# All matrix products in 64x64 array tiles, in pairs that exchange their row halves

## The chip, the cores and the metric

One core of a Trainium2 chip runs the kernel. TensorE (PE) multiplies, ScalarE (ACT) and VectorE (DVE) empty its results from the eight PSUM banks, GpSimd (POOL) and SyncE (SP) issue DMAs. The metric is the device time of one execution in microseconds (us), as a median of several runs.

## What is computed

Attention without a softmax, and then an MLP mixer over its result; 8 batch items, 12 heads, 448 tokens, 64 channels a head.

```python
def _attn_ref(q, k, v):
    S = q.shape[2]
    scale = 1.0 / np.sqrt(q.shape[-1])
    scores = scale * np.matmul(q, k.transpose(0, 1, 3, 2))
    attn = np.maximum(scores, 0.0) ** 2 / S
    return np.matmul(attn, v)
# x: the heads side by side, (8, 448, 768)
def _moe_ref(x, w_tok1, w_tok2, w_ch1, w_ch2):
    xt = x.transpose(0, 2, 1)
    h = np.maximum(xt @ w_tok1, 0.0) @ w_tok2      # 448 -> 256 -> 448
    u = x + h.transpose(0, 2, 1)
    h2 = np.maximum(u @ w_ch1, 0.0) @ w_ch2        # 768 -> 1536 -> 768
    return u + h2
```

Inputs and output are float32; the kernel computes in bfloat16 with float32 sums.

## The kernel before

The 96 pairs of batch item and head are worked off in 24 steps of four heads (`NS`), three steps to a batch item. Tokens are numbered as seven blocks of 64 (`KC`, `KP`): token 7p + c is place p of block c.

The stages of a step, with the names that the planner and the lines carry:

- T (L526): q and k are transposed, on PE in the first nine steps, by DMA later.
- S (L577): scores of one token block for four heads, four matmuls in 64x64 array tiles ("a quad"), into two banks. ACT or DVE take the relu (L309, L311), DVE squares (L611).
- V (L629): the product with v, 7 quads, into two banks; scaled into `xT` (L659, L661).
- X: x is transposed back to token rows, on PE in the first six steps (L714), by DMA later.
- t1 (L751): first token product, full 128x128 matmuls of 256 columns, tokens padded to 512 so that each of four K steps has 128 rows. Relu into `r1`.
- t2 (L786): second token product, one bank for each of two head pairs; DVE adds x and writes `uT` (L798).

Then, per batch item, come the channel products: C1 (L842), for each of 12 output blocks six accumulating 128x128 matmuls of 448 columns into one bank, then a relu into `r2` (L309); and C2 (L913), for each of 28 x 2 output tiles twelve matmuls of 384 columns into one bank, then DVE adds u (L947), and SP stores the result. A chain of C1 or C2 is one unit that nothing interrupts.

What sets the order: each operation of each stage is an `Op` with dependencies, duration, number of banks and rank, and a `Planner` walks through a model of time and gives out the operations, engine by engine. The program then runs in this fixed order, with semaphores between the engines. The model reckons 0.093 us for a change of PE's tile shape (`shape` "s" for 64x64, "m" for 128x128), and so runs several S or V operations on end (`run`, `WAIT`) before it goes to the full-size units, and begins such a run only with enough free banks (`OPEN`, `SPARE`). Loads on POOL are a fixed list. Small matmuls on a tile of zeros (L432, L436) keep PE busy in the first 16 us.

Of the kernel before, what the change touches and what calls it, by code (L numbers as in the profile page):

```python
# [17 lines left out]
WAIT, SPARE, OPEN = 0.1, 1, 6  # L18
# [5 lines left out]
class Op:  # L24
    def __init__(self, name, eng, emit, deps=(), **kw):
        self.name, self.eng, self.emit = name, eng, emit
        self.deps = [d for d in deps if d is not None]
        self.on = None
        self.start = self.seen = None
        self.banks = 0  # L30
        self.bank = []
        self.frees = None
        self.rank = 0
        self.shape = None
        self.lag = 0.0
        self.work = None
        self.late = None
        self.durs = None
        self.batch = None
        self.step = 0  # L40
        self.spare = 0
        self.gate = None
        self.first = self.then = None
        self.__dict__.update(kw)
# [5 lines left out]
class Planner:  # L50
# [10 lines left out]
    def done(self, o):  # L61
        for d in o.users:
            d.left -= 1
            d.at = max(d.at, o.seen)
            if d.left == 0:
                self.open[d.pool].append(d)

    def run(self, todo, reserve, least, lanes=8, held=0.0, fill=None):
        for n, o in enumerate(self.ops):
# [3 lines left out]
            o.pool = "FLEX" if o.durs else "UNIT" if o.shape == "m" else "PE" if o.shape else o.eng  # L73
# [11 lines left out]
        banks = [0.0] * 7 + [held]  # L85
        ring = 0.0
        landed = {"POOL": [], "SP": []}
        todo = list(todo)
        shape, owed, run = None, 0.0, False
# [6 lines left out]
        idle = 0.0  # L96
        while left:
            for e in ("SP", "POOL"):
# [23 lines left out]
                left -= 1  # L122
            for e in ("ACT", "DVE"):
# [23 lines left out]
                o.emit(o)  # L147
                self.log.append((t, e, o.name, o.durs[e]))
# [5 lines left out]
            if free["PE"] <= t:  # L154
                o = None

                def fits(c, spare=0):
                    at = t + (0.093 if shape not in (None, c.shape) else 0.0)
                    return c.ready(at) and sum(b <= at for b in banks) >= c.banks + max(spare, c.spare if c.then and c.then.left > 1 else 0)

                pick = None
                for u in self.open["UNIT"]:
                    if fits(u) and (pick is None or (u.rank, u.n) < (pick.rank, pick.n)):
                        pick = u
                spare = 0 if pick is None else SPARE
                head = todo[0] if todo else None
                if head and head.step < TIGHT and not head.ready(t):
                    head = next((u for u in todo[1:LOOK] if u.ready(t)), head)
                if pick is not None and pick.rank < 0:
                    o = pick  # L170
                    run = False
                elif run and head and fits(head, spare):
                    o = head
                elif run and head and idle < WAIT:
                    pass
                else:
                    run = False
                if o is None and not run:
                    if pick is None:
                        o = next((u for u in todo[:12] if fits(u)), None)  # L180
                    elif head and owed <= 0.0 and fits(head, max(0, OPEN - head.banks)):
                        o = head
                    else:
                        o = pick
                if o is None:
                    idle += step
                else:
                    at = t + (0.093 if shape not in (None, o.shape) else 0.0)
                    idle = 0.0
                    if o.shape == "m":  # L190
                        owed = max(owed - o.dur, -2.0)
                    else:
                        run = True
# [13 lines left out]
                    for k in order:  # L207
                        banks[k] = 1e9
                    self.open[o.pool].remove(o)
# [12 lines left out]
def kernel(  # L222
# [22 lines left out]
    SP = 512  # L245
# [9 lines left out]
    EARLY1, EARLY2, SPARE1 = 3, 3, 3  # L255
# [10 lines left out]
    xTs = [sbuf.tile([128, 2, SP], BF16, name=f"xT{i}") for i in range(NX)]  # L266
    wt1 = sbuf.tile([128, 4, DT], BF16, name="wt1")
# [7 lines left out]
    x_sbs = [sbuf.tile([128, 2, 4, 128], BF16, name=f"x_sb{i}") for i in range(2)]  # L275
# [4 lines left out]
    outs = sbuf.tile([128, NO, DM], FP32, name="out_sb")  # L280

# [6 lines left out]
    VFROM, ASPLIT = 3, 3  # L288
# [18 lines left out]
    def relu(o, out, ps):  # L307
        if o.on == "ACT":
            nc.scalar.activation(out, ps, AF.Relu)  # L309
        else:  # L310
            nc.vector.tensor_scalar(out=out, in0=ps, scalar1=0.0, scalar2=None, op0=ALU.max)  # L311

    def copy(o, out, ps):
        if o.on == "ACT":
            nc.scalar.activation(out, ps, AF.Copy)
        else:
            nc.vector.tensor_copy(out, ps)  # L317

    def freed(u, i=None):
        return lambda o: u.bank if i is None else [u.bank[i]]  # L320

# [55 lines left out]
    def load_wt1():  # L377
        w = moe_w_tok1.rearrange("(p c) j -> c p j", c=KC)
        got = []
        for c2 in range(2):  # L380
            n = (KC + 1 - c2) // 2

            def emit(o, c2=c2, n=n):
                nc.gpsimd.dma_start(
                    out=wt1[64 * c2 : 64 * (c2 + 1), :n, :],
                    in_=w[c2::2].rearrange("c p j -> p c j"),
                )

            got.append(add(Op(f"wt1.{c2}", "POOL", emit, dur=0.6, work=0.9)))
        return got  # L390
# [50 lines left out]
    nc.vector.memset(wt1, 0.0)  # L441
    for x in xTs:
        nc.vector.memset(x[:, :, S:], 0.0)

# [175 lines left out]
    def value(s):  # L620
# [35 lines left out]
        def evict(o, half):  # L656
            dst = xTs[s % NX][:, half, :S]
            if o.on == "ACT":
                nc.scalar.activation(dst, u.ps[half][:, :S], AF.Copy, scale=float(alpha2))  # L659
            else:  # L660
                nc.vector.tensor_scalar(  # L661
                    out=dst, in0=u.ps[half][:, :S], scalar1=float(alpha2), scalar2=None, op0=ALU.mult
# [22 lines left out]
    def mixing(s):  # L685
# [4 lines left out]
        if s >= XDMA:  # L690
# [5 lines left out]
                        out=x_sb.rearrange("p a c d -> p (a c) d"),  # L696
                        in_=xTs[s % NX].rearrange("p a n -> p (a n)"),
# [6 lines left out]
            ready = xback[s] * 2  # L704
        else:
            ready = [None, None]
            xback[s] = []
            for lo, hi in ((0, 1), (1, 2)) if s < ASPLIT else ((0, 2),):

                def emit_x(o, lo=lo, hi=hi):  # L710
                    o.ps = bank(o, 0, "x_ps").bitcast(BF16).rearrange("p (a c d) -> p a c d", a=2, c=4)
                    for a in range(lo, hi):
                        for c in range(4):
                            nc.tensor.matmul(  # L714
                                o.ps[:, a, c, :],
                                lhsT=xTs[s % NX][:, a, c * 128 : (c + 1) * 128],
                                rhs=ident,
# [6 lines left out]
                u = add(Op(f"X{s}.{lo}", "PE", emit_x, xe[s][lo:hi], shape="m", banks=1, dur=0.22 * (hi - lo), rank=1))  # L724
                xback[s].append(u)
                units.append(u)
                n = 512 * (hi - lo)
                cp = add(
                    Op(
                        f"xc{s}.{lo}",  # L730
                        "DVE",
                        lambda o, lo=lo, hi=hi, u=u: copy(o, x_sb[:, lo:hi], u.ps[:, lo:hi]),
                        [u] + old,
                        durs={"ACT": 0.05 + n / 1200, "DVE": 0.067 + n / 1920},
                        slack=0.4,
                        rank=1,
                        frees=freed(u),
                    )
                )
                for a in range(lo, hi):  # L740
                    ready[a] = cp

        r1 = r1s[s % 2]
        t1e[s], r1_op = [], [None, None]
        for lo, hi in ((0, 1), (1, 2)) if s < ASPLIT else ((0, 2),):

            def emit_1(o, lo=lo, hi=hi):
                o.ps = bank(o, 0, "t1_ps").rearrange("p (j n) -> p j n", j=JC)
                for j in range(JC):
                    for c in range(4):  # L750
                        nc.tensor.matmul(  # L751
                            o.ps[:, j, lo * 128 : hi * 128],
                            lhsT=wt1[:, c, j * 128 : (j + 1) * 128],
                            rhs=x_sb[:, lo:hi, c, :],
                            start=(c == 0),
                            stop=(c == 3),
                        )

            t1 = add(
                Op(f"t1.{s}.{lo}", "PE", emit_1, ready[lo:hi] + wt1_ops, shape="m", banks=1, dur=0.436 * (hi - lo), rank=1)  # L760
            )
            t1e[s].append(t1)
            units.append(t1)
            n = 256 * (hi - lo)
            ev = add(
                Op(
                    f"r1.{s}.{lo}",
                    "ACT",
                    lambda o, lo=lo, hi=hi, t1=t1: relu(
                        o, r1[:, :, lo * 128 : hi * 128], t1.ps[:, :, lo * 128 : hi * 128]  # L770
                    ),
                    [t1] + [ue.get((s - 2, a)) for a in range(2)],
                    durs={"ACT": 0.05 + n / 1200, "DVE": 0.067 + n / 960},
                    slack=0.3,
                    rank=0,
                    frees=freed(t1),
                )
            )
            for a in range(lo, hi):
                r1_op[a] = ev  # L780
        for a in range(2):

            def emit_2(o, a=a):
                o.ps = bank(o, 0, "h_ps")
                for j in range(JC):
                    nc.tensor.matmul(  # L786
                        o.ps[:, :S],
                        lhsT=r1[:, j, a * 128 : (a + 1) * 128],
                        rhs=wt2[:, j, :],
                        start=(j == 0),  # L790
# [272 lines left out]
```

## Time and profile before

| what | us |
|---|---|
| median of 3 runs (358.99 to 359.59) | 359.37 |
| the profiled execution | 359.65 |
| its span, first to last instruction | 357.8 |
| PE busy | 351.8 |
| DVE busy | 232.5 |
| ACT busy | 202.0 |
| POOL busy | 84.3 |

The span leaves out 1.85 us of the profiled execution. Busy is the time in which an instruction of the engine runs; matmuls overlap in the record, so PE's 351.8 says that it nearly always had work, not how fast it went. The costliest stages on PE by busy time are C2 (115.2 us), C1 (115.0), S (48.0) and V (37.2). The DMA engines' mean busy share is nine tenths or more in nearly all of the first three quarters of the span.

### The profile page before, as it was taken

The page shows a single profiled execution, that of the slowest core. Times are in us where ns is not written, and L with a number is a line of the kernel's source. Part 1 is how long each engine was busy: PE and PEld are TensorE (multiplying, and loading weights), DVE is VectorE, ACT ScalarE, POOL GpSimd, SP SyncE. Part 2 cuts the span into 40 slices and gives each one's busy share as a digit, 9 for nine tenths or more (in the row PEclk, how much of TensorE's full clock was granted, in tenths as well). Part 3 has the DMA queues.
Part 4 walks back from the last instruction along what each step waited for, and adds up shares of the span by engine and source line. Part 5 has one row for each costly group of instructions (what it writes and reads, how often), then busy time and mean ns, then how long its engine had stood idle before and what let it go on. Part 6 is the DMA issues. An engine that isn't in the chain of part 4 may idle for free.

```text
span 357.8 us, 8801 instructions
## 1 busy us (share of the span) xinstructions
PE 351.8 (98%) x3516; PEld 196.8 (55%) x3516; DVE 232.5 (65%) x430; ACT 202.0 (56%) x419; POOL 84.3 (24%) x141
## 2 busy tenths in 40 slices
PE   8999999999999999999999999999999999999995
PEld 5655465555555555555455555455455555565564
DVE  3999387796677986877588696687676682031032
ACT  4998784467853577457674278644675344402400
POOL 8732524403132130333123213203000000000000
PEclk9999999999999999999999999999999999999999
DMA  8999999999999999999998999999951444033024
GB/s 138 192 213 188 175 210 201 173 169 187 134 134 166 178 165 128 152 174 204 161 134 160 164 191 158 132 129 199 153 104 33 110 103 90 15 76 88 2 65 111
DMA packets 98122, 50.62 MB, mean 141 GB/s; under 512 B 72801, under 2 KB 93857, under 8 KB 98081
## 3 DMA queue, kind: packets, MB, share of 16 engines
q1 hardware_dynamic: 74320, 28.49, 46.5%
q0 software_dynamic: 23600, 21.47, 43.3%
q8 instruction: 27, 0.44, 0.5%
q14 instruction: 15, 0.11, 0.2%
q10 hardware_dynamic: 160, 0.10, 0.1%
HBM read 43.38 MB, written 11.01 MB: 152 GB/s over the span
## 4 chain that ended last, share of the span: by engine, by line
PE 95%; DVE 3%; ACT 1%; issue 0%; ACTq 0%
PE m_ps L913 31%; PE m_ps L842 31%; PE sc_ps L577 10%; PE acc_ps L629 9%; PE t_ps L751 6%; PE h_ps L786 5%; PE warm_ps L432 2%; DVE sq L611 1%; ACT sq L309 1%; PE kqT_ps L526 1%; PE x_ps L714 1%; DVE x_sb L317 0%; DVE uT_sb L798 0%; DVE xT L661 0%; DVE kqT L317 0%
## 5 line engine op out<-in xcount | busy, mean ns | idle before, releaser
L309 ACT ACTIVATE sq<-sc_ps 128x448 bf16<-128x448 f32 x254 | 118.9, 563 | 58.4 <-PE sc_ps L577 58.4
L913 PE MATMUL m_ps<-wc,r_sb 128*128 128x384 bf16 (+2 forms) x684 | 115.2, 323 | 0.0
L842 PE MATMUL m_ps<-uT_sb,wc 128*128 128x448 bf16 x576 | 115.0, 353 | 0.0
L611 DVE TENSOR_TENSOR sq<-sq 128x896 bf16<-128x896 bf16 x168 | 98.0, 618 | 3.2 <-ACT sq L309 1.7
L913 PEld LDWEIGHTS <-r_sb 128*128 128x128 bf16 x684 | 65.6, 98 | 44.5 <-issue 3.8
L309 ACT ACTIVATE r_sb<-m_ps 128x448 bf16<-128x448 f32 x96 | 52.6, 550 | 64.5 <-PE m_ps L842 64.4
L842 PEld LDWEIGHTS <-wc 128*128 128x128 bf16 x576 | 55.2, 98 | 52.2 <-issue 3.8
L311 DVE TENSOR_SCALAR sq<-sc_ps 128x448 bf16<-128x448 f32 x82 | 49.1, 620 | 31.3 <-PE sc_ps L577 31.3
L947 DVE TENSOR_TENSOR out_sb<-m_ps,u_sb 128x384 f32<-128x384 f32 (+2 forms) x57 | 31.3, 549 | 54.2 <-PE m_ps L913 54.0
L577 PE MATMUL sc_ps<-kqT 64*64 64x448 bf16 x672 | 48.0, 357 | 0.2 <-ACT sq L309 0.2
L362 POOL DMA_DIRECT2D k_raw<-in_k_dram x30 | 17.8, 600 | 100.9 <-DMA kqT<-kqi 51.3
L362 POOL DMA_DIRECT2D v_raw<-in_v_dram x48 | 28.8, 609 | 42.9 <-PE sc_ps L577 33.9
L798 DVE TENSOR_TENSOR uT_sb<-h_ps,xT 128x448 bf16<-128x448 f32 x48 | 27.6, 617 | 15.2 <-PE h_ps L786 15.2
L629 PE MATMUL acc_ps<-sq,v_raw 64*64 64x448 bf16 x672 | 37.2, 350 | 0.2
L577 PEld LDWEIGHTS <-kqT 64*64 64x64 bf16 x672 | 17.0, 105 | 21.9 <-issue 14.3
L629 PEld LDWEIGHTS <-v_raw 64*64 64x64 bf16 x672 | 19.9, 107 | 13.7 <-issue 2.7
L751 PE MATMUL t_ps<-x_sb,wt 128*128 128x256 bf16 (+1 forms) x216 | 25.2, 262 | 0.0
L751 PEld LDWEIGHTS <-wt 128*128 128x128 bf16 x216 | 17.6, 98 | 8.6 <-issue 6.4
L786 PE MATMUL h_ps<-wt,r_sb 128*128 128x448 bf16 x96 | 22.1, 353 | 0.1
L661 DVE TENSOR_SCALAR xT<-acc_ps 128x448 bf16<-128x448 f32 x24 | 14.9, 622 | 7.2 <-PE acc_ps L629 7.2
L362 POOL DMA_DIRECT2D q_raw<-in_q_dram x30 | 18.2, 620 | 3.5 <-issue 2.0
L659 ACT ACTIVATE xT<-acc_ps 128x448 bf16<-128x448 f32 x24 | 13.2, 551 | 5.7 <-PE acc_ps L629 5.1
(36 smaller groups left out, 122.8 us busy)
## 6 DMA issues: line engine op xcount, KB each, us to landing
out_dram<-out_sb SPq DMA_DIRECT2D x54, 192.0 KB, 3.4
v_raw<-in_v_dram POOLq DMA_DIRECT2D x48, 112.0 KB, 6.5
wc<-in_moe_w_ch_dram POOLq DMA_DIRECT2D x6, 768.0 KB, 13.4
k_raw<-in_k_dram POOLq DMA_DIRECT2D x30, 112.0 KB, 4.0
q_raw<-in_q_dram POOLq DMA_DIRECT2D x30, 112.0 KB, 5.2
k_raw<-in_k_dram POOLq DMA_DIRECT2D x8, 224.0 KB, 9.8
q_raw<-in_q_dram POOLq DMA_DIRECT2D x8, 224.0 KB, 8.5
u_sb<-uT_sb SPq DMA_TRANSPOSE x48, 3.9
```

The lines of the kernel that those rows point to most:

```text
L309: nc.scalar.activation(out, ps, AF.Relu)
L311: nc.vector.tensor_scalar(out=out, in0=ps, scalar1=0.0, scalar2=None, op0=ALU.max)
L362: ins = nc.gpsimd.dma_start(out=raws[t][s % NR][64 * half : 64 * (half + 1)], in_=src[b, h0 : h0 + 2].rearrange("e (p c) d -> p e (c d)", ...
L577: nc.tensor.matmul(o.ps[z][64 * y : 64 * (y + 1), :S], lhsT=kT[rows, half, c, :], rhs=qT[rows, half, :, :], start=True, stop=True, skip_gr ...
L611: lambda o: nc.vector.tensor_tensor(out=buf, in0=buf, in1=buf, op=ALU.mult),
L629: nc.tensor.matmul(o.ps[half][64 * e : 64 * (e + 1), :S], lhsT=r[rows, e, c * D : (c + 1) * D], rhs=sq[rows, e, :], start=(c == 0), stop=( ...
L751: nc.tensor.matmul(o.ps[:, j, lo * 128 : hi * 128], lhsT=wt1[:, c, j * 128 : (j + 1) * 128], rhs=x_sb[:, lo:hi, c, :], start=(c == 0), sto ...
L786: nc.tensor.matmul(o.ps[:, :S], lhsT=r1[:, j, a * 128 : (a + 1) * 128], rhs=wt2[:, j, :], start=(j == 0), stop=(j == JC - 1),)
L798: nc.vector.tensor_tensor(out=uTs[bb % 2][:, 2 * i + a, off : off + S].rearrange("n (c p) -> n c p", c=KC), in0=t2.ps[:, :S].rearrange("n ...
L842: nc.tensor.matmul(o.ps[:, :S], lhsT=wc1[:, g, e * 128 : (e + 1) * 128], rhs=uT[:, g, off : off + S], start=(g == 0), stop=(g == CC - 1), ...
L913: nc.tensor.matmul(o.ps[:, :m], lhsT=r2[:, e, t * 128 : (t + 1) * 128], rhs=wc2[:, e, cols], start=(e == 0), stop=(e == EC - 1), skip_grou ...
L947: nc.vector.tensor_tensor(out=out_sb[:, cols].rearrange("n (g d) -> n g d", d=128), in0=u.ps[:, :m].rearrange("n (g d) -> n g d", d=128), ...
```

## The change

- C1, C2 and t2 run in 64x64 tiles. Two outputs (two blocks of C1, both halves of a C2 tile, both head pairs of t2) are made together in two banks: in the first phase the upper 64 rows of the contraction are summed for output 0 and the lower 64 for output 1, in the second phase the rows are exchanged. Each former matmul becomes four instructions and a quarter of the array.
- Between the phases a bank changes its row tile. The first matmul of the second phase waits for an operation of DVE or ACT that has seen the end of the first phase; for each such turn there is a one-column memset or activation (`touch`). The planner may put other work between phases and keeps at most two pairs of C1 or C2 open (`PAIRS`).
- t1 no longer pads: `x_sb` holds one head pair in the upper and one in the lower 64 partitions, the weights are loaded to both halves, and 7 K steps of 64 rows run for both pairs at once, 128 columns each. `xT` is laid out by token block; X on PE becomes seven quads of 64x64 transposes and is copied by DVE and ACT.
- All these carry shape "s". The last batch item's C1 (`ALONE1`) and the last four output tiles of C2 (`ALONE2`) stay full-size.
- The planner's rule for S and V: they go ahead when the units are not owed time and S, V and T together hold at most four banks (`MOST`), instead of running on end.

```diff
+    def chain(name, parts, emit, deps, slot, **kw):
+        us = []
+        for n, (phase, lo, hi) in enumerate(parts):
+            before = us[-1] if us else None
...
+                if before.phase != phase:
+                    add(
+                        Op(
+                            f"{name}.{n}.turn",
+                            "DVE",
+                            lambda o, before=before: touch(o, before),
+                            [before],
+                            durs={"ACT": 0.06, "DVE": 0.07},
+                            slack=0.0,
+                            rank=-5,
+                            turns=u,
...
+    def touch(o, before):
+        if o.on == "ACT":
+            o.ins = nc.scalar.activation(specks[0], specks[0], AF.Copy)
+        else:
+            o.ins = nc.vector.memset(specks[1], 0.0)
+        order_after(o.ins, before.tail, "row tiles change banks")
...
+    def turned(o, ins):
+        if o.mark is not None and o.tail is None:
+            order_after(ins, o.mark.ins, "row tiles change banks")
+        o.tail = ins
+
+    def quads(o, weights, moving, n, name, has=lambda x, k: True):
+        o.ps = o.first.ps if o.first else [bank(o, i, name) for i in range(2)]
+        lo, hi = o.span
+        for k in range(lo, hi):
+            for x in range(2):
+                rows = slice(64 * x, 64 * (x + 1))
+                i = x ^ o.phase
...
+                for y in range(2):
+                    ins = nc.tensor.matmul(
+                        o.ps[i][64 * y : 64 * (y + 1), :n],
+                        lhsT=weights(i, k)[rows, 64 * y : 64 * (y + 1)],
+                        rhs=moving(i, k)[rows],
...
     def load_wt1():
...
+        def emit(o, h):
+            nc.gpsimd.dma_start(
+                out=wt1[64 * h : 64 * (h + 1)], in_=moe_w_tok1.rearrange("(p c) j -> p c j", c=KC)
...
+            for j in range(JC):
+                for c in range(KC):
+                    for a in range(2):
+                        rows = slice(64 * a, 64 * (a + 1))
+                        for y in range(2):
+                            nc.tensor.matmul(
+                                o.ps[a][64 * y : 64 * (y + 1), j, :],
+                                lhsT=wt1[rows, c, j * 128 + 64 * y : j * 128 + 64 * (y + 1)],
+                                rhs=x_sb[rows, c, :],
...
+        us = chain(f"t2.{s}", [(0, 0, JC), (1, 0, JC)], emit_2, lambda lo, hi: r1_op + wt2_ops, 0.189, rank=0)
...
+            parts = [(0, 0, 4), (1, 0, 4), (1, 4, CC), (0, 4, CC)] if early else [(0, 0, CC), (1, 0, CC)]
+            us = chain(f"C1.{b}.{e}", parts, emit, deps, 0.189, rank=2, batch=b)
...
+            parts = [(0, 0, 8), (1, 0, 8), (1, 8, EC), (0, 8, EC)] if early else [(0, 0, 6), (0, 6, EC), (1, 0, 6), (1, 6, EC)]
+            us = chain(f"C2.{n}", parts, emit, lambda lo, hi: done + [wc2_ops[e] for e in range(hi)], 0.1625, rank=2, batch=b)
...
+                    if u.first is None and u.pair and begun >= PAIRS and u.batch is not None:
+                        continue
...
+                room = head and (not more or sum(b > t and k for b, k in zip(banks, small)) + head.banks <= MOST)
...
+                elif head and room and (owed <= 0.0 or pick is None) and fits(head):
                     o = head
-                elif run and head and idle < WAIT:
-                    pass
```

## The prediction

> **What bounds the kernel now.** I read the page first: busy shares, clock, chain that ended last, groups. The clock is full in all 40 slices, so no time is lost to throttling.
>
> ```profile
> span 357.8 us, 8801 instructions
> PE 351.8 (98%) x3516; PEld 196.8 (55%) x3516; DVE 232.5 (65%) x430; ACT 202.0 (56%) x419; POOL 84.3 (24%) x141
> ...
> PE 95%; DVE 3%; ACT 1%; issue 0%; ACTq 0%
> PE m_ps L913 31%; PE m_ps L842 31%; PE sc_ps L577 10%; PE acc_ps L629 9%; PE t_ps L751 6%; PE h_ps L786 5%; PE warm_ps L432 2%; DVE sq L611 1%; ACT sq L309 1%; PE kqT_ps L526 1%; PE x_ps L714 1%; DVE x_sb L317 0%; DVE uT_sb L798 0%; DVE xT L661 0%; DVE kqT L317 0%
> ```
>
> TensorE (PE) is 98% busy and 95% of the chain: only what shortens PE's own stream shortens the kernel. But a busy PE isn't PE at its rate, so next comes PE's timeline in the middle of the run (start, length, engine, line, tile shape, count):
>
> ```profile
> 121.19 2.11 PE L913 MATMUL m_ps<-wc,r_sb 128*128 128x384 bf16 x12
> 123.23 0.76 PE L577 MATMUL sc_ps<-kqT 64*64 64x448 bf16 x12
> 123.92 3.58 PE L842 MATMUL m_ps<-uT_sb,wc 128*128 128x448 bf16 x18
> 127.43 0.57 PE L577 MATMUL sc_ps<-kqT 64*64 64x448 bf16 x8
> 127.84 1.49 PE L629 MATMUL acc_ps<-sq,v_raw 64*64 64x448 bf16 x28
> 129.16 0.55 PE L577 MATMUL sc_ps<-kqT 64*64 64x448 bf16 x8
> 129.64 1.05 PE L751 MATMUL t_ps<-x_sb,wt 128*128 128x256 bf16 x8
> ```
>
> Starts are what to read, since ends are modelled. The V group (L629), 28 matmuls in 64x64 tiles, holds PE from 127.84 to 129.16: 1.32 us for 7 quads of four, 0.189 us a quad, as much as one 128x128 matmul of 448 columns (below). So 64x64 tiles lose no rate. The C1 group (L842), 18 matmuls, holds 123.92 to 127.43: 3.51 us, where 18 x 0.189 are 3.41; 0.1 us are left at its end, where the tile shape changes. From the starts of single matmuls: C1 to C1 189 ns, C1 to S (128x128 to 64x64) 282 ns in all of 24 places; C2 to C2 163 ns, C2 to S 256 ns; S to C1 282 ns. A change of tile shape costs 93 ns, both ways. The stream has 116 of them: 10.8 us.
>
> PE's time from its first matmul start (1.06 us) to its last (353.95) then splits into: matmuls at their rates, 330.7 (C1 576 x 0.189 = 109.0; C2 109.2; S and V 168 quads each, 31.8 + 31.8; t1 168 x 0.109 + 48 x 0.056 = 21.0; t2 96 x 0.189 = 18.2; X 48 x 0.056 = 2.7; T 3.7; warm and fill 3.4); changes 10.8; the rest 11.4. Of the rest 9.0 lie in the first 40 us (some 2 in the half-rate warm matmuls), 2.3 between 40 and 300, none later. PE hardly waits for anybody after the start. The table by stretches says who limits the start (busy us of each engine and count; last: clock, DMA share, GB/s):
>
> ```profile
> 10.00:40.00 30.00, 28.73 (x491) 16.82 (x493) 25.01 (x49) 27.36 (x63) 14.94 (x23) 1.00 1.21 196
> 40.00:100.00 60.00, 60.00 (x820) 33.18 (x813) 46.18 (x83) 41.27 (x84) 18.33 (x30) 1.00 1.16 176
> 100.00:200.00 100.00, 100.00 (x904) 54.76 (x902) 77.72 (x142) 58.43 (x122) 28.56 (x48) 1.00 1.13 160
> ```
>
> From 10 to 40 us ACT is busy 27.4 of 30 and DVE 25.0; later they are at 58 to 78%.
>
> [...] V runs a quad with its four loads in 189 ns, and the 64x64 transposes (L526, also four loads a quad) start on average every 10 ns, 40 ns a quad. Weight loads don't bind.
>
> **The change, part by part.** Counts for the changed kernel come from the order of its instructions on each engine.
>
> 1. Changes of tile shape: 116 become 8 (warm-up, and once at the end). 108 x 93 ns = 10.0 us saved. All are on PE's path.
> 2. C1, C2 and t2 in quads: C1 504 quads + 72 full matmuls, C2 576 quads + the same tail, t2 96 quads: same columns, same 0.189 and 0.163 a quad. Nothing, if C2's 384-wide quad holds 163 ns: eight instructions in 163 ns, where the transposes do eight in 40.
> 3. t1: 336 quads of 128 columns at 56 ns (the 128-wide full matmul's rate; the transposes' 40 shows that the loads fit) = 18.8 against 21.0: 2.2 saved. X (six steps only): 42 quads at 40 ns = 1.7 against 2.7: 1.0 saved. Sum of 1 to 3: 13.2 us.
> 4. Turns. 42 C1 pairs, 24 C2 pairs and 24 t2 pairs exchange row halves once, the earliest C1 and C2 pair twice: 92 turns, each a wait of an LDWEIGHTS on PE for a one-column memset (53, DVE) or activation (39, ACT) that itself waits for the last matmul before. Need, from pieces of the trace: the drain of a 448-wide matmul, 0.354 recorded less 0.189 to the next start = 0.165; about 0.04 to a waiting DVE (354.17 to 354.21 at the end); the small op, which no row shows (the smallest DVE row, 128 columns, has 0.29, the POOL constants' memsets 0.10; between 0.06 and 0.29, I take 0.15); about 0.06 back to PE (ACT end 16.04, PE weight load 16.10). Some 0.42 us, plus up to one operation in front of it on DVE or ACT (0.45 to 0.62), plus the weight load, no longer pulled ahead, 0.1. So 0.45 to 1.1. Cover: I counted the matmul time that stands between the two halves of each chain. 7 turns have 0.19 to 0.38 us, 11 have 0.57 to 0.65, 11 have 0.76 to 0.98, 63 have 1.13 or more. The 7 stall about 0.4 each (2.8), the 11 about 0.1 (1.1), the rest almost nothing: 4.0. Low end 2; high end 9, if the 11 + 11 stall 0.3 each as well. Behind the waiting LDWEIGHTS stands all of PE's stream; behind the memset on DVE stand squares and evictions, but it is placed where the matmul should be done.
> 5. Banks. A pair holds two banks for 2.3 us (C1) or 3.9 (C2) and what runs in between, where a chain held one for 1.1 or 2.0. At most two pairs are open, S keeps four banks. PE then waits on evictions closer to their end; 0 to 3 us, I take 0.5.
> 6. The start. Before the first C1 PE has 19.7 us of matmuls and changes to do instead of 22.9. But ACT (91%) and DVE (83%) set the pace there, x now is copied on both engines and t2 has turns; the token weights are loaded to both halves (0.46 MB more; at 196 GB/s 2.3 us of DMA ahead of the channel weights, whose third part lands at 33.4 us, with C1 from 32.9). Of the 3.2 us won there 0 to all are lost; I take 2.0. Without that cover (the weights late on top) 2.3 more.
> 7. Hidden: an eighth less in each x transpose DMA, the second r1 eviction per step, three memsets less on DVE, a strided xT write; PE waits for none of them after the start. POOL's queue keeps its order and SP's its issues. The tail after the last matmul (3.85 us) is unchanged: the last 12 C1 and 4 C2 tiles stay full-size.
>
> Sum: 13.2 - 4.0 - 0.5 - 2.0 = 6.7 us. On the profiled execution: 359.65 (span 357.8 and 1.85 around it) - 6.7 = 352.95; the median shown is 0.28 lower (359.37), so I forecast 352.7.
>
> **Rivals.** (a) The forecast, 349 to 357: chance 0.57. (b) Nearly all arrives: waits as well hidden as in before, where 40 to 300 us lost only 2.3; only the short covers stall (2) and the start loses nothing: 359.4 - 13.2 + 2 = 348.2, with no stall at all 346.2. For it speaks the median cover of 1.16 us. Chance 0.26. (c) Slower: the turns. If each of the 92 costs over 0.12 us on average ((13.2 - 2.0) / 92), the gain is gone; at 0.2 us it is 359.4 - 11.2 + 18.4 = 366.6. It takes ACT and DVE that run about half an operation late, so that covers of 0.8 to 1.3 fail too. Against it: they idle 22 to 42% after 40 us, and the 63 long covers exceed the whole need. For it: DVE is at 77%, strictly in order, and each touch waits for PE in turn. Also on this side, with a small share: PE's instruction stream grows from 7034 to 16586, and its 27 fetches of 16 KB (the queue line of the page, 0.44 MB) to some 65, one every 6 us beside a DMA share above 1.1; in before fetches 5.5 to 7 us apart occur without a gap in PE. Chance 0.14. (d) Gain and waits cancel: 0.03. That the changes of shape stay is excluded by the order.
>
> **How the numbers follow.** Two tenths of a per cent, 0.7 us, is about what a measurement tells from no change. Faster: (a) + (b) = 0.83; same 0.03; slower 0.14. The range leaves out (c) and little else: down to 346.5, near (b) with no stall; up to 359.0, where the costs of steps 4 to 6 together reach 12.8 of their 15.2 at the high ends (9 + 3 + 3.2).
>
> **What would show it.** PE's starts: C1 quads 189 ns, C2 163, t1 56, and 8 changes of 93 ns. If C2's quads take longer, step 2 is wrong. PE's and PEld's waits on the small DVE and ACT operations should sum to 4 us, mostly in few turns of short cover; over 11 there means (c). The first C1 near 31 us; after 33 means step 6 was too mild. The last V group should end about 50 us before the end.

## The result: slower, mostly because PE's instructions come too late

| | before | after |
|---|---|---|
| median, us | 359.31 (358.99 to 359.59, 4 runs) | 384.39 (383.61 to 391.35, 4 runs) |
| profiled execution | 359.65 | 384.41 |
| its span | 357.8 | 382.6 |

The ratio is 1.069, with a 95% interval of 1.067 to 1.071; it leaves out the execution of 391.35 us, which ran at a lower granted clock (0.973 on average, 0.985 to 0.991 in the other three). The forecast was 352.7, its range 346.5 to 359.0.

The page of the kernel after, from the span over the slices to the DMA queues and the chain (the queue lines give packets, MB, share of 16 engines):

```profile
span 382.6 us, 18420 instructions
PE 354.2 (93%) x8292; PEld 272.7 (71%) x8292; DVE 238.4 (62%) x489; ACT 214.8 (56%) x473; POOL 84.2 (22%) x141
...
PEclk9996998999999999999999999999999999999999
DMA  9999999975488989989989999979997492243114
...
q8 instruction: 65, 1.06, 1.2%
...
PE 83%; issue 7%; DVE 5%; ACT 4%; DVEq 0%; ACTq 0%
```

PE's share of the chain fell from 95 to 83%. "issue", time in which an engine waits for nothing that the profile shows, rose from 0 to 7% (some 26 us), and the clock dips in two places. The queue q8 is the one the page calls "instruction"; before, its line read:

```profile
q8 instruction: 27, 0.44, 0.5%
```

Whom does PE wait for? The waits of PE in after, then those of its weight loads (engine, tile, line, who released it: us in total, times, longest):

```profile
PE m_ps L416 <- issue: 7.7, 7, 1.6
PE acc_ps L722 <- issue: 5.2, 2, 3.8
PE x_ps L807 <- issue: 2.9, 2, 1.6
PE t_ps L845 <- issue: 2.8, 4, 1.3
...
PE h_ps L416 <- DVE speck L390: 0.6, 2, 0.4
```

```profile
PEld L416 <- DVE speck L390: 3.5, 7, 0.8
...
PEld L416 <- ACT speck L388: 1.3, 4, 0.6
```

The suspected turns (the small operations on `speck`) cost 4.8 us of weight-load waits. The 18.6 us of "issue" in the four upper lines are new: in before PE has no such wait at all. Where are they? PE's timeline of after around the longest (start, length, engine, line, tile shape, count; in brackets idle time and releaser), and around one in mid-run:

```profile
26.75 0.76 PE L722 MATMUL acc_ps<-sq,v_raw 64*64 64x448 bf16 x10
31.32 1.33 PE L722 MATMUL acc_ps<-sq,v_raw 64*64 64x448 bf16 x10 [3.81 <-issue]
32.07 1.32 PE L416 MATMUL h_ps<-wt,r_sb 64*64 64x448 bf16 x8
```

```profile
126.68 1.29 PE L416 MATMUL m_ps<-wc,r_sb 64*64 64x384 bf16 x24
127.65 0.51 PE L670 MATMUL sc_ps<-kqT 64*64 64x448 bf16 x4
127.84 0.51 PE L416 MATMUL m_ps<-wc,r_sb 64*64 64x384 bf16 x6
129.90 1.00 PE L416 MATMUL m_ps<-wc,r_sb 64*64 64x384 bf16 x18 [1.54 <-issue]
```

Both stalls fall inside one unit and inside a quad of four: the V group stops after ten matmuls, the C2 chain after six. Nothing that a unit waits for can stop it there. Numbering all matmuls from 0 gives the pattern: every such stall lies between matmul 93 and 94 of a group of 128, whatever these compute. With their weight loads 128 matmuls are 256 instructions; 65 packets for some 16,590 instructions (8292 pairs and a few more) are 255 each, and a packet is 16,384 bytes. So PE stops at the borders of its blocks of instructions. Putting the packets of q8 beside the borders gives this (us; "crossed" is the start of a block's first matmul, "last before the border" that of its last one, "resumed" that of the next block's first):

| crossed | packet of the next block | last before the border | resumed | stall |
|---|---|---|---|---|
| 25.12 | 28.87 to 29.82 | 27.16 | 31.32 | 4.1 |
| 123.21 | 127.36 to 128.49 | 128.03 | 129.90 | 1.8 |
| 321.21 | 321.53 to 322.49 | 326.10 | 326.25 | 0 |

One block's packet starts after PE has entered the block before it: after 1.69 us in the median, 3.85 at the 90th percentile (up to 310 us of the span), about 0.3 us after 310 us, where the DMA share has fallen to 0.35 from 1.00 before. The packet takes about 1.0 us (0.99 in the median). At all 17 stalls over 0.45 us PE resumed 1.23 to 1.54 us after its packet's end. So, as an estimate from these sums, a block has to last some 4 us in the median case, over 6 in bad ones. In before blocks last 13.45 us in the median and 5.7 at the shortest. In after the median is 5.15, and where X, t1 and transposes lie in them, whose matmuls are short, 2.0 to 4.5.

With starts, matmul rates and 93 ns a shape change (in before C1 to S 282 ns instead of 189), PE's time from first to last matmul start splits as follows:

| us | before | after | difference |
|---|---|---|---|
| matmuls at their rates | 330.7 | 326.95 | -3.7 |
| changes of tile shape | 10.8 | 0.75 | -10.05 |
| stalls at block borders | 0.8 | 25.05 | +24.3 |
| extra time at half clock, after the start | 0 | 4.3 | +4.3 |
| the start: 16 matmuls of 256 columns at 213 ns instead of 109, rest of the first 40 us | 8.9 | 9.8 | +0.9 |
| gaps and small remainders after 40 us | 1.7 | 10.8 | +9.1 |
| sum | 352.9 | 377.65 | +24.8 |

The expected gain, 13.75 us, is all there. The borders alone eat it nearly twice. The half clock comes with two of the stalls: 2.3 us into the one at 27.5 the granted clock falls to half for 6.83 us, and again at 63.89, 0.5 us after a stall of 1.65, for 3.41; in before it is full from 6.4 us, where its record begins, to the end of the span. The stretches by time (from:to, us; busy us and count of PE, PEld, DVE, ACT, POOL; clock, DMA share, GB/s) show where PE is short of work:

```profile
0.00:40.00 40.00, 31.67 (x759) 20.85 (x760) 26.63 (x55) 27.94 (x62) 23.01 (x40) 0.91 1.12 188
40.00:100.00 60.00, 52.03 (x1464) 40.88 (x1467) 38.54 (x82) 35.39 (x76) 13.64 (x22) 0.97 0.91 139
100.00:200.00 100.00, 94.86 (x2298) 75.88 (x2294) 68.90 (x142) 61.55 (x138) 25.02 (x43) 1.00 1.01 140
200.00:300.00 100.00, 96.80 (x2348) 79.74 (x2344) 65.01 (x132) 62.37 (x139) 22.52 (x38) 1.00 1.01 141
```

Between 40 and 300 us PE was busy throughout in before; now 16.3 us are missing, half of them before 100. Neither DVE nor ACT is near its limit there, and both are less busy than before in the first 100 us. The DMA engines are: their share is 0.91 to 1.01.

### The profile page after: what moved, and what is told of

Same layout as the page of the kernel before. It is cut to its first block, busy times and chain, and to the rows that moved or that the text cites. A ratio compares the mean times of both kernels' runs of the same rounds, so it can differ in the third digit from the quotient of the medians.

```text
span 382.6 us, 18420 instructions
## 1 busy us (share of the span) xinstructions
PE 354.2 (93%) x8292; PEld 272.7 (71%) x8292; DVE 238.4 (62%) x489; ACT 214.8 (56%) x473; POOL 84.2 (22%) x141
## 4 chain that ended last, share of the span: by engine, by line
PE 83%; issue 7%; DVE 5%; ACT 4%; DVEq 0%; ACTq 0%
PE m_ps L416 48%; PE acc_ps L722 8%; PE sc_ps L670 6%; PE t_ps L845 6%; PE m_ps L1066 4%; PE h_ps L416 4%; PE m_ps L935 3%; ACT sq L331 2%; DVE sq L704 1%; PE warm_ps L529 1%; DVE uT_sb L882 1%; PE kqT_ps L619 1%; DVE kqi L339 1%; PE x_ps L807 1%; DVE out_sb L1016 1%
## 5 line engine op out<-in xcount | busy, mean ns | idle before, releaser
L331 ACT ACTIVATE sq<-sc_ps 128x448 bf16<-128x448 f32 x312 | 149.2, 558 | 29.1 <-PE sc_ps L670 28.3
L416 PEld LDWEIGHTS <-r_sb 64*64 64x64 bf16 x2688 | 103.8, 107 | 23.5 <-issue 8.7
L416 PE MATMUL m_ps<-wc,r_sb 64*64 64x384 bf16 x2304 | 113.0, 323 | 5.0 <-issue 4.3
L416 PE MATMUL m_ps<-uT_sb,wc 64*64 64x448 bf16 x2016 | 111.4, 350 | 4.3 <-issue 3.4
L416 PEld LDWEIGHTS <-wc 64*64 64x64 bf16 x2016 | 74.5, 107 | 30.6 <-issue 8.0
L331 ACT ACTIVATE r_sb<-m_ps 128x448 bf16<-128x448 f32 x48 | 26.1, 545 | 37.3 <-PE m_ps L416 18.5
L333 DVE TENSOR_SCALAR r_sb<-m_ps 128x448 bf16<-128x448 f32 x48 | 29.8, 621 | 21.6 <-PE m_ps L416 11.8
L670 PEld LDWEIGHTS <-kqT 64*64 64x64 bf16 x672 | 32.9, 108 | 10.9 <-issue 4.5
L416 PE MATMUL h_ps<-wt,r_sb 64*64 64x448 bf16 x384 | 32.2, 360 | 0.8 <-DVE speck L390 0.6
L845 PE MATMUL t_ps<-x_sb,wt 64*64 64x128 bf16 x1344 | 26.5, 220 | 3.1 <-issue 2.8
L845 PEld LDWEIGHTS <-wt 64*64 64x64 bf16 x1344 | 25.1, 109 | 5.5 <-issue 3.9
L753 ACT ACTIVATE xT<-acc_ps 128x448 bf16<-128x448 f32 x24 | 13.2, 551 | 26.6 <-PE acc_ps L722 25.7
```

What stands on the lines that cost most here:

```text
L331: o.ins = nc.scalar.activation(out, ps, AF.Relu)
L333: o.ins = nc.vector.tensor_scalar(out=out, in0=ps, scalar1=0.0, scalar2=None, op0=ALU.max)
L416: ins = nc.tensor.matmul(o.ps[i][64 * y : 64 * (y + 1), :n], lhsT=weights(i, k)[rows, 64 * y : 64 * (y + 1)], rhs=moving(i, k)[rows], star ...
L670: nc.tensor.matmul(o.ps[z][64 * y : 64 * (y + 1), :S], lhsT=kT[rows, half, c, :], rhs=qT[rows, half, :, :], start=True, stop=True, skip_gr ...
L845: nc.tensor.matmul(o.ps[a][64 * y : 64 * (y + 1), j, :], lhsT=wt1[rows, c, j * 128 + 64 * y : j * 128 + 64 * (y + 1)], rhs=x_sb[rows, c, : ...
```

## The experiments

Two questions: are the turns or the instruction supply behind the loss, and where do the 9 us of gaps come from? A time without a range is one run; the kernel before, run beside them, took 359.1 to 359.7. "Borders", "half clock" and "gaps" are measured as in the table above, gaps being starts over 60 ns late, away from borders, after 40 us: 12.2 us in after, about 0 in before.

**No exchange.** After, without the exchange of rows and its waits; PE's order stays the same.

```diff
-                i = x ^ o.phase
+                i = x
...
-        if o.mark is not None and o.tail is None:
-            order_after(ins, o.mark.ins, "row tiles change banks")
```

> The changed kernel in which the second phase keeps the row halves of the first (both phases sum the same half of the contraction, so half of each sum is left out), PE's order as before, and PE waits for no turn. Theory A (PE's instruction supply: the stalls at every 128th matmul, 25.1 us, and the half clock after two of them, 4.3 us): the time stays within 374 to 384 us; at most the gaps elsewhere after 40 us, 12.2 us, go, and the stalls at every 128th matmul remain at 20 us or more. Theory B (the turns make it slow): the time falls by 20 us or more, to 364 or less.

Measured: 387.94 us, above the 374 to 384 expected and not faster than after. PE waits for no `speck` any more; its largest waits are these:

```profile
PE t_ps L843 <- issue: 6.5, 3, 3.4
PE m_ps L414 <- issue: 5.9, 7, 1.4
PE acc_ps L720 <- issue: 3.8, 2, 3.5
```

Borders 26.6 us, half clock 9.6, gaps 9.8. The turns aren't the cause of the loss: without them gaps fall by 2.4 us, but the stalls at the 128th matmuls stay, 1.5 us more, and the half clock takes 5.3 more. It is one execution, at a mean granted clock of 0.973.

**Fewer loads.** After, without the q, k and v loads from step 4 on: PE's matmuls unchanged, less DMA traffic. If the packets, 1.69 us after the crossing in the median, are late because the DMA engines are busy, they now come sooner.

```diff
+                if s >= NR:
+                    return
```

> The changed kernel without the loads of q, k and v from step 4 on (the steps compute with the data of the first four). Orders on PE, ACT, DVE and SP unchanged; POOL issues nothing there. Theory A (each 16 KB block of PE instructions is fetched when the block before is begun[...]): the sum at every 128th matmul falls from 25.1 us to under 8, the half clock goes, and the time is 352 to 366 us. Theory B (turns and evictions): the DMA load doesn't matter, 380 us or more.

Measured: 370.03 us, above the 352 to 366 expected. The slices of DMA, and PE's waits:

```profile
DMA  8999940135443848549561764458623863134023
```

```profile
PE acc_ps L726 <- issue: 2.5, 1, 2.5
PE t_ps L849 <- issue: 2.2, 3, 0.9
PE x_ps L811 <- issue: 1.5, 1, 1.5
...
PE m_ps L416 <- issue: 1.1, 1, 1.1
```

The borders cost 8.1 us instead of 25.05, all of it before 78 us; the packets start 0.68 us after the crossing in the median, not 1.69. As many fetches over quieter engines stall for a third of the time: most of the stalling here is a wait for busy DMA engines. The half clock, expected to go, is still there (10.24 us from 26.68 on, beside the longest stall that is left), and gaps stay, 13.3.

**The control.** The same edit in the kernel before.

> The kernel before without the loads of q, k and v from step 4 on, the control to the same edit of the changed kernel. Theory A: its instruction blocks come in time, PE waits for no DMA, nothing changes: 357.5 to 360 us. If it gains several us too, the gain of the edit in the changed kernel is no evidence for the instruction supply.

Measured: 359.74 us. The loads as such cost before nothing, so what the edit gave after came through something that before doesn't have.

**More instructions in before.** Each C1, C2 and t2 matmul in four column pieces: 128x128 tiles, the old order, no turns.

```diff
+                for z in range(4):
                     nc.tensor.matmul(
-                    o.ps[:, :S],
+                        o.ps[:, z * S // 4 : (z + 1) * S // 4],
```

> The kernel before, with every matmul of C1, C2 and t2 cut into four pieces of a quarter of the columns: 7584 matmuls instead of 3516, same products, no turns, no new layout, same order. The pieces add 1356 x 3 x 2.5 ns = 10 us at most at the rates of the trace, if the weight loads keep up. Theory A: on top of that, stalls at every 128th matmul of 10 to 25 us appear, and the time is 375 to 395 us. Theory B (turns): no such stalls, 359 to 370 us.

Measured: 379.94 us, with 59 fetches. PE's waits now have the entry that before lacked:

```profile
PE m_ps L846 <- issue: 4.8, 3, 1.7
PE kqT_ps L526 <- issue: 1.7, 1, 1.7
...
PE m_ps L918 <- issue: 0.8, 2, 0.6
```

Stalls of 1.7 to 1.9 us stand at 44, 50, 70 and 229 us, all at the same index modulo 128: borders 7.8, half clock 1.6, gaps 0.1. The shorter pieces themselves cost 9.9 (49 ns instead of 47.25 and 43 instead of 40.75, four to a matmul; the 2.5 ns a piece taken for it are about what before's rates leave beside the columns: by 56 ns for 128 and 189 for 448 it is 2.8). So the instruction count alone makes the stalls. They are fewer than the 10 to 25 us expected. The blocks are more even: 6.3 us in the median and 4.3 at the shortest, where after has 5.15 and 2.0. And without touching the order no gaps appear.

**Half the instructions of C1, C2, t2 and t1.** After, with the two column halves of a tile merged: tiles of 64 rows by 128 columns in C1, C2, t2 and t1.

> The changed kernel with C1, C2, t2 and t1 in tiles of 64 rows by 128 columns: the two column halves of a quad in one matmul, 5268 matmuls instead of 8292, turns and order the same. Theory A: the blocks of 128 matmuls last half as long again, the stalls at every 128th matmul fall under 5 us. If going between 64x64 and 64x128 tiles costs nothing, the time is 345 to 356 us; if it costs 93 ns like the other change of shape, 287 of them add 27 us, 370 to 382 us. Theory B: as the changed kernel or slower, with the gaps at the turns as large.

Measured: 389.97 us, above the 370 to 382 expected. Only three stalls over 0.3 us are left at borders (1.1, 0.9, 2.0), with 41 fetches, and the clock stays full. But the timeline shows a new cost:

```profile
122.73 1.14 PE L415 MATMUL m_ps<-wc,r_sb 64*128 64x384 bf16 x12
123.80 0.38 PE L669 MATMUL sc_ps<-kqT 64*64 64x448 bf16 x4
124.12 1.15 PE L415 MATMUL m_ps<-wc,r_sb 64*128 64x384 bf16 x12
```

Six C2 pairs take 6 x 0.163 = 0.98 us, but S starts 1.07 after them; its one quad takes 0.19, but C2 starts 0.32 later. Going from 64x128 to 64x64 cost 93 ns and back mostly 117 to 120, and there are 287 such changes, some 30 us. The result can't be read as a time without stalls, but it shows what fewer instructions do to the borders. The two shapes have the same 64 rows, and going between them cost at least as much as the 93 ns between 64x64 and 128x128 in before.

**t1 alone.** Before with only t1 and X in 64x64 tiles, held back up to 10 us for a moment when that shape is current.

> The kernel before with one part of the change alone: X and t1 in 64x64 tiles with the new layout of x and of the token weights (C1, C2 and t2 full-size, no turns); the planner may hold X and t1 back up to 10 us so that they follow S or V. 4764 matmuls, 112 changes of shape. By the rates of the trace t1 saves 2.2 us, X 1.0 and four changes 0.4. Theory A (instruction supply): 128 matmuls last 9 us on average, so only the densest blocks stall; 355 to 359 us. If the stalls come with t1's dense 56 matmuls as such: 362 us or more.

Measured: 370.74 us (370.13 to 371.52), ratio 1.032 (1.030 to 1.034). So not the 355 to 359 us came, but the other case, 362 or more. In the timeline:

```profile
29.00 0.55 PE L778 MATMUL h_ps<-wt,r_sb 128*128 128x448 bf16 x2
31.93 0.91 PE L778 MATMUL h_ps<-wt,r_sb 128*128 128x448 bf16 x2 [2.38 <-issue]
```

A t2 chain stands still, 2.4 us idle. Four stalls lie at borders, all at the same index modulo 128 as in after: 1.3 us at 25, 2.5 at 29, 0.7 at 62, 1.6 at 131, the last two inside t1, borders 5.7 in all. The clock is at half from 31.5 to 34.9. That doesn't explain all: the run is 11.5 us slower where 3.6 were to be saved, so 15 are lost, and borders with the half clock (about 1.5) make 7.2 of them. The rest, some 8 us, lies in the first 40 us and in gaps after them; it was not taken apart. With 37 fetches instead of 27 it isn't the mean rate that fails, but the few blocks in which 28, 56 and again 28 matmuls go by in 0.3 to 0.8 us each.

**Only one load.** After, with only step 0's q, k and v loaded, to see what the gaps are.

> The changed kernel with the loads of q, k and v of step 0 alone, every step computing with them; the weights are loaded as ever. Orders on PE, ACT, DVE and SP unchanged. Theory A: the stalls at every 128th matmul fall under 4 us and the half clock goes, so the time is 384.4 less 25.1, less 4.3 and plus what is left: 354 to 360 us. If the time stays over 366 us, most of the loss has another cause.

Measured: 367.98 us (367.13 to 368.82), ratio 1.025 (1.021 to 1.028). Borders 7.6, nearly all up to 75.3 us, but gaps 12.9, as many as in after; 3.41 us at half clock are left. The expected 354 to 360 was missed: the gaps have another cause than DMA traffic.

**One load, no exchange.** Both edits together.

> The changed kernel with the loads of step 0 alone and without the exchange (both phases sum the same half of the contraction, half of each sum is left out, PE waits for no turn). Against the one with the exchange the difference is what the 92 turns cost once the instruction supply is out of the way: 2 to 5 us less, as the waits on the small operations in the trace of the changed kernel sum to 4.3 us. Theory B: 15 us or more.

Measured: 367.08 us (366.18 to 367.97), ratio 1.022 (1.019 to 1.025). The turns are worth 0.9 us between the medians, less than the 2 to 5 expected, and the two ranges overlap. That may be too low: this execution has 6.83 us at half clock, the one with turns 3.41, which can hide up to 1.7 us, and gaps fall by 2.0 to 10.9. Even so most of the gaps are not the turns.

What is left is the order. In after's timeline at the change of batch item, with ACT and PE:

```profile
141.57 2.29 ACT L331 ACTIVATE sq<-sc_ps 128x448 bf16<-128x448 f32 x5 [1.11 <-PE sc_ps L670]
141.62 1.41 PE L670 MATMUL sc_ps<-kqT 64*64 64x448 bf16 x12
...
143.04 0.90 PE L416 MATMUL m_ps<-uT_sb,wc 64*64 64x448 bf16 x12
```

Three S quads, 0.57 us of matmuls, hold PE for 1.42, while ACT empties their banks one after another at 0.46 us each. The planner has used up its C1 and C2 work and can only put S quads on end.

**More work in reserve.** After, with the work of C1 and C2 that the planner keeps in hand for this place raised from 10 to 14 us. It is the complete kernel.

```diff
-    RES, LEAST = (0.0, 10.0), (0.4, 0.05, 0.4)
+    RES, LEAST = (0.0, 14.0), (0.4, 0.05, 0.4)
```

> The changed kernel with one planner number changed: it holds back 14 us of C1 and C2 work for a batch item's border instead of 10, so that S quads stand less often three or four in a row (7 such places fewer in the order). Theory: the gaps after 40 us that aren't at every 128th matmul (12.2 us) come from S waiting for evictions where the planner has run out of C1 and C2 work; they fall to 5 to 9 us. The stalls at every 128th matmul stay near 25 us, 20 to 30. Time 376 to 388 us. If the gaps stay at 12, they have another cause.

Measured: 375.46 us. Gaps 6.8 instead of 12.2, borders 20.2, half clock 3.25. Clumps of 10 to 12 S matmuls fell from ten to five, those of 16 from two to none.

**More in reserve, one load.**

> The same number, and the loads of step 0 alone (every step computes with the data of step 0). Theory: with the instruction supply eased the gaps show undisturbed: 5 to 9 us after 40 us where the same kernel with the number 10 had 12.9, and the time is 361 to 366 us (368.0 there).

Measured: 361.96 us, 6.0 less than with the old reserve; gaps fall from 12.9 to 7.4. The gaps follow the reserve, with and without the loads. Here borders (6.1) and half clock (3.5) are still in it; without these 9.6 it would be 352.4, worked out and not run: the forecast's size, in a kernel that loads q, k and v only once.

**Longer runs in before.** If 116 changes cost 10.8 us, could before's planner make fewer?

```diff
-WAIT, SPARE, OPEN = 0.1, 1, 6
+WAIT, SPARE, OPEN = 0.5, 0, 6
```

> The kernel before with two planner numbers changed: a run of S and V waits up to 0.5 us instead of 0.1 for its next one, and keeps no spare bank. 96 changes of tile shape instead of 116, same 3516 matmuls. 20 x 93 ns = 1.9 us saved, less what PE waits in the longer runs: 357.5 to 360.5 us. Nothing at every 128th matmul.

Measured: 373.91 us (373.72 to 374.25), ratio 1.040 (1.039 to 1.042). There are 96 changes, 1.9 us less, but S now stands behind S: 16.8 us of gaps, 13.2 of them from one S matmul to the next, waiting for banks. The weight loads of S say so:

```profile
PEld L577 <- issue: 19.9, 64, 0.7
```

In before that entry was 14.3 us in 42 waits. The expectation was wrong. No version tried beats the kernel before; the best complete one of the change is the larger reserve, at 375.46.

## Why the prediction was wrong

- Steps 1 and 3 (changes of shape, t1 and X) and 2 (quads): right. The 13.2 us came as 13.75. Away from borders the quads of C1 and t2 start every 189 ns, those of C2 every 163 and those of t1 every 56, as taken; those of X every 32, where 40 were taken. In the working, T at 3.7 us and its 504 transposes at 10 ns on average (5.0 us) don't fit each other; the average has pauses in it, and the sum doesn't use it.
- Step 4 (turns): right in size, 4.0 foreseen, 4.8 by the waits of the weight loads, and worth little when removed (no exchange: not faster; with one load: 0.9 us, up to 2.6 if the longer half clock there is counted out). Before the small operations DVE and ACT sat idle for 36.7 us until PE released them. That the exchange of rows needs such a wait was the author's assumption; no run has the exchange without it. The touch itself is cheaper on DVE and dearer on ACT than the 0.15 taken. The small operations in after (engine, operation, tile, count: shortest/median/longest ns, first to last start):

```profile
L390 DVE MEMSET speck<- x53: 59/59/59, 21.9 to 347.9; 128x1 bf16 x53
L388 ACT ACTIVATE speck<-speck x39: 197/205/265, 33.4 to 327.9; 128x1 bf16<-128x1 bf16 x39
```

- Step 5 (banks): mis-sized, 0.5 taken, 3 at most. Gaps and remainders grew by 9.1 us, which also hold the turns. The step asked what two open pairs do to the banks. It didn't ask what the new order does when no pair is left to open: the old rule ran S and V on end only with free banks, the new one relies on C1 and C2 work, and at the change of batch item that work is gone. The reserve moved the gaps by 5.4 and 5.5 us, which shows this for about half of them; the other half I didn't take apart.
- Step 6 (start): about right without the supply: +0.9 us in the first 40. The first C1 came at 39.6 and not near 31, but stalls at borders (6.4 us up to 38.3) and the half clock account for most of that. So the sign named for a step too mild, a first C1 after 33, came from another cost.
- The failed step is in rival (c): "Also on this side, with a small share: PE's instruction stream grows". The count was right to the piece: some 65 fetches, one every 6 us, beside a DMA share above 1.1. The reason for dismissing it, that "in before fetches 5.5 to 7 us apart occur without a gap in PE", compared the shortest distance in before with the mean distance in after. The shortest block in after lasts 2.0 us, and half last under 5.15. A stall here depends on the single block: delay of the packet (1.69 us in the median, up to 4.5), packet (1), resumption (1.4) against the time in which PE uses up 128 matmuls. That step was worth 24.3 us and 4.3 more through the clock; it was in the sum with nothing, and in the chances with a part of 0.14 whose named mechanism was another one.

What is shown: that the stalls are at block borders, that more instructions alone bring them (column pieces), that fewer loads take two thirds of them away, and that the turns are a few us at most. What stays open: what exactly calls for a packet (the earliest start when PE is still 19 matmuls short of the border, in before up to 3.2 us early), how long it then waits, and whether some other place for the loads would cure the stalls. In before the first nine packets, up to 77 us, start 1.5 to 4.0 us after the crossing, as late as in after: its blocks are long enough to hide it. No run moved the loads without removing them.

## What to carry to other kernels

Count instructions, not only array time, when matmuls are split (here 65 packets of them instead of 27 came with 24.3 us of stalls more): find the packets of the instruction queue in the trace, take PE's time per block at the densest place, not on average, and compare it with the time from crossing to resumption under that stretch's DMA load. Stalls marked "issue" that fell in the middle of a unit, at a fixed count of instructions, were the supply here. When an order is changed so that long units cover short ones, look at the place where the long units run out.

## What the runs showed of the hardware that was not expected

- The instruction queue moved one packet of 16,384 bytes for each 128 matmuls with their weight loads, 65 in after and 27 in before. In after a packet started 1.69 us in the median after PE had entered the block before (19 matmuls short of it at the earliest, 4.5 us after it at the latest), with fewer loads 0.68; it took about 1.0 us, and at the stalls PE resumed 1.23 to 1.54 us after its end.
- The clock fell to half for 6.83 and 3.41 us in after (starts 34.13 apart) and for 10.24 with fewer loads: two, one and three times 3.41. In after the first stretch set in 2.3 us after PE's last matmul ended, the second 0.5 us after the end of a stall of 1.65 us. A stall of 1.64 us at 78.4 brought none; what sets it off is open.
- Mixing 64x64 and 64x128 tiles was not free: 93 ns for a change from 64x128, mostly 117 to 120 for one to it, some 30 us for 287.
- The supply stalls of after cost more than their length: of the 29.3 us put down to them, 4.3 are matmuls that were in time but ran at half clock.
